# First batch's running sums on TensorE instead of VectorE scans, and the list of words written out anew

## The chip, the cores and the metric

The kernel runs on one core of one Trainium2 chip. A core has five engines that run their own instruction lists in order and wait for one another by semaphores: TensorE (matrix products, PE in the profile, with its weight loads PEld), VectorE (DVE), ScalarE (ACT), GpSimd (POOL) and SyncE (SP), which here issues most DMA transfers. The metric is the device time of one execution in microseconds; the median of three runs of the kernel before is 524.56 us (524.19 to 525.32).

## The reference

Two blocks follow one another, all in float32, with 4 batches, 8 heads of 48 channels and 768 tokens.

```python
f = 1.0 / (1.0 + np.exp(-f_logit))
for t in range(S):
    state = f[:, :, t, :, None] * state + np.einsum('bhd,bhe->bhde', k[:, :, t], v[:, :, t])
    y[:, :, t] = np.einsum('bhd,bhde->bhe', q[:, :, t], state)
x = y.transpose(0, 2, 1, 3).reshape(4, 768, 384)
u = x + np.real(np.fft.fft(np.fft.fft(x, axis=1), axis=2))
un = (u - u.mean(-1)) / sqrt(u.var(-1) + 1e-6)
out = u + np.maximum(un @ w_ch1, 0.0) @ w_ch2        # 384 -> 1536 -> 384
```

So each head is a gated linear recurrence with a decay for every channel and token, and then come a Fourier mixing over tokens and channels and a feed-forward block with a residual.

## The kernel before, in words

**Attention.** The work is cut into 16 units: unit u is one batch and two heads (batch u // 4), with the channels of both heads on 112 partitions and the 768 tokens along the row. A unit is treated in 6 chunks of 128 tokens. What the recurrence needs is, for each channel, the running sum of ln(1 + exp(-f)) over the tokens of a chunk, started anew at each chunk at -10. In `attention` (line 364 on) ScalarE makes the logarithm (lines 372, 373); VectorE's scan of line 379 makes the running sum W over the whole row, where the tile `bound` (22 everywhere, -10 at a chunk's first token) is the second operand of its `min` and so restarts the sum; line 380 adds the last token's logarithm and keeps the total of each chunk in `deep`. ScalarE takes exp(-W) and exp(W) (383, 384), and VectorE multiplies them into the queries and the keys (391, 392). Then come, on TensorE: the scores inside half chunks (`sc`, line 400), masked by VectorE into `at` (404); the scores between halves (576), copied to `ao`; the transposed keys (`st`, 538); the outputs `y` from scores and values (559); the state sums of each chunk (`ds`, 599), scanned over chunks by VectorE (`stt`, 607); the read-out of the state into `y` (616); and the transposition of the output (`yt`, 636), which ScalarE copies to the token-major x. VectorE folds x for the Fourier mixing (`fold`, 663 to 669; after the second and fourth unit of a batch also `xs`, `se`, `xc`, `ce`, 678 to 687).

**Mixing and feed-forward.** For each batch `fnet` makes four products `z` with the cosine and sine tables (724) and three `mix` products (743); each row block is normalised, transposed (`pt`, 782) and put through the feed-forward block in three pairs of row blocks. The first batch uses plain products: `up` (871, twelve for a pair, each with a relu on ScalarE), then `po` (880); its other two pairs and all later ones use a seven-product form for the second matrix (`fx`, `fz`, 894), and later batches a fifteen-product form for the first one (`ub`, 840). The two weight matrices arrive as float64 in 24 blocks: a word `r` fetches one (310), a word `C` turns it into float32 with one ScalarE, two VectorE and one GpSimd instruction (281 to 285). Three fetched blocks have room at a time, so a fetch waits for the GpSimd addition three blocks earlier.

**What sets the order.** Nothing is scheduled by the machine: the string `ORDER` is a list of words that is read from left to right, and each word emits a piece of the program, which every engine gets in this order. A number is the next step of that unit (its generator's next `yield`), K its transposed keys, L a load on SyncE's queue, F and H steps of the mixing, P a step of the feed-forward block, T and S the tables' loads and sorting, V and c a second reading of the weights for their smallest sizes, M the final test of whether the fast path was accurate. A word `D` emits eight products of the tile `bound` with itself into a spare part of the `y` tile (lines 189 to 194, 192): nobody reads them, they only occupy TensorE. The kernel before has 21 of them, 20 before the first z product.

**Buffers.** f, q and k tiles are shared by units (`home`), scores, keys, states and outputs take turns in two double banks of PSUM (`ps_a`, tag sc), the mixing in two banks (`ps_f`, tag f), and all units write to one `y`.

## Time and profile before

| | |
|---|---|
| median of three runs | 524.56 us (524.19 to 525.32) |
| profiled execution, first to last instruction | 526.3 us |
| mean granted TensorE clock | 0.974 |
| TensorE matmuls busy | 494.9 us (94%) |
| TensorE weight loads busy | 453.4 us (86%) |
| VectorE busy | 378.3 us (72%) |
| ScalarE busy | 218.4 us (42%) |
| GpSimd busy | 58.8 us (11%) |
| dummy products (line 192) | 14.6 us |
| scans of line 379 | 28.0 us, 16 of them |
| first z product of the first batch | at 59.5 us |

The profile is of one execution, and its span lies 1.7 us above the median of the runs, which are not profiled. Busy shares are means over stages with different limits: they are read stage by stage. A float32 product of the program stands as two matmul records in the trace, a transpose as one. "Issue" in the chain of waits is time in which an engine waited for nothing that the profile shows. The granted clock is 1.00 at full speed and 0.50 at half.

### The profile page before, as it was taken

The page shows a single profiled execution, that of the slowest core. Times are in us where ns is not written, and L with a number is a line of the kernel's source. Part 1 is how long each engine was busy: PE and PEld are TensorE (multiplying, and loading weights), DVE is VectorE, ACT ScalarE, POOL GpSimd, SP SyncE. Part 2 cuts the span into 40 slices and gives each one's busy share as a digit, 9 for nine tenths or more (in the row PEclk, how much of TensorE's full clock was granted, in tenths as well). Part 3 has the DMA queues.
Part 4 walks back from the last instruction along what each step waited for, and adds up shares of the span by engine and source line. Part 5 has one row for each costly group of instructions (what it writes and reads, how often), then busy time and mean ns, then how long its engine had stood idle before and what let it go on. Part 6 is the DMA issues. An engine that isn't in the chain of part 4 may idle for free.

```text
span 526.3 us, 13807 instructions
## 1 busy us (share of the span) xinstructions
PE 494.9 (94%) x5854; PEld 453.4 (86%) x5854; DVE 378.3 (72%) x746; ACT 218.4 (42%) x520; POOL 58.8 (11%) x85
## 2 busy tenths in 40 slices
PE   5878599999999999999999999999999999999994
PEld 4757388866899889999999999999999999999994
DVE  3598989989955368688588776779776667465571
ACT  5567368656331542453435523550431404031220
POOL 3045033551001000000001000000001000010100
PEclk9789699999999999999999999999999999999998
DMA  8957837575010230103212012120610312220200
GB/s 222 268 147 206 210 109 214 161 221 158 6 55 30 68 97 17 54 21 114 77 55 84 1 55 72 46 63 23 206 43 15 107 47 81 83 91 8 84 11 27
DMA packets 20650, 48.15 MB, mean 91 GB/s; under 512 B 3426, under 2 KB 6179, under 8 KB 20579
## 3 DMA queue, kind: packets, MB, share of 16 engines
q1 hardware_dynamic: 19474, 43.63, 29.5%
q0 software_dynamic: 1104, 3.54, 1.8%
q8 instruction: 48, 0.79, 0.6%
q14 instruction: 24, 0.19, 0.1%
HBM read 42.44 MB, written 4.72 MB: 90 GB/s over the span
## 4 chain that ended last, share of the span: by engine, by line
PE 87%; DVE 6%; issue 2%; ACT 2%; DMA 1%; POOL 0%; SPq 0%; DVEq 0%; ACTq 0%
PE ub L840 23%; PE fx L894 16%; PE fz L894 11%; PE up L871 9%; PE z L724 5%; PE y L559 4%; PE mix L743 3%; PE y L616 2%; PE sc L400 2%; PE ds L599 2%; PE po L880 2%; PE yt L636 2%; PE pt L782 1%; PE st L538 1%; PE y L192 1%
## 5 line engine op out<-in xcount | busy, mean ns | idle before, releaser
L849 DVE TENSOR_TENSOR h<-h,ub 128x512 f32<-128x512 f32 x81 | 55.2, 687 | 33.5 <-PE ub L840 24.5
L692 POOL DMA_INDIRECT out_dram<-x,place x16 | 16.4, 1024 | 357.6 <-DVE x L944 224.3
L847 ACT ACTIVATE h<-ub 128x512 f32<-128x512 f32 x54 | 31.9, 591 | 42.3 <-PE ub L840 42.3
L871 PE MATMUL up<-unT,w 128*128 128x256 f32 x216 | 49.4, 382 | 0.0
L840 PE MATMUL ub<-wide,w 128*128 128x128 f32 x360 | 45.0, 276 | 2.3 <-DVE wide L814 2.3
L894 PE MATMUL fx<-block,h 128*128 128x192 f32 x264 | 46.9, 328 | 0.0
L894 PE MATMUL fx<-w,h 128*128 128x192 f32 x264 | 45.5, 327 | 0.0
L840 PEld LDWEIGHTS ub<-wide,w 128*128 128x128 f32 x360 | 42.4, 192 | 3.4 <-PE pt L782 1.3
L871 PEld LDWEIGHTS up<-unT,w 128*128 128x128 f32 x216 | 40.1, 190 | 5.9 <-ACT h L873 0.4
L851 ACT ACTIVATE h<-h 128x512 f32<-128x512 f32 x45 | 28.4, 631 | 38.1 <-DVE h L849 37.7
L894 PEld LDWEIGHTS fx<-block,h 128*128 128x128 f32 x264 | 43.2, 190 | 0.5 <-DVE x L911 0.2
L894 PEld LDWEIGHTS fx<-w,h 128*128 128x128 f32 x264 | 42.7, 190 | 0.4 <-issue 0.2
L285 POOL TENSOR_TENSOR w<-w,raw 128x384 uint32<-128x384 uint32 x24 | 29.4, 1228 | 72.3 <-DVE w L284 39.1
L840 PE MATMUL ub<-unT,w 128*128 128x128 f32 x288 | 37.0, 275 | 0.0
L840 PEld LDWEIGHTS ub<-unT,w 128*128 128x128 f32 x288 | 34.6, 192 | 0.0
L783 ACT COPY unT<-pt 128x384 f32<-128x384 f32 x24 | 11.4, 484 | 46.8 <-PE pt L782 46.6
L840 PE MATMUL ub<-unT,wide 128*128 128x128 f32 x216 | 29.1, 278 | 0.0
L840 PE MATMUL ub<-wide 128*128 128x128 f32 x216 | 28.6, 275 | 0.1
L873 ACT ACTIVATE h<-up 128x256 f32<-128x256 f32 x36 | 13.9, 385 | 33.6 <-PE up L871 22.0
L840 PEld LDWEIGHTS ub<-unT,wide 128*128 128x128 f32 x216 | 26.4, 192 | 0.5
L840 PEld LDWEIGHTS ub<-wide 128*128 128x128 f32 x216 | 26.3, 192 | 0.3 <-PE ub L840 0.3
L379 DVE TENSOR_TENSOR_SCAN W<-g,bound 112x768 f32<-112x768 f32 x12 | 21.0, 1747 | 6.7 <-ACT g L373 6.7
(194 smaller groups left out, 1000.1 us busy)
## 6 DMA issues: line engine op xcount, KB each, us to landing
raw<-in_w_ch_dram SPq DMA_DIRECT2D x24, 384.0 KB, 5.1
v<-in_v_dram SPq DMA_DIRECT2D x16, 288.0 KB
k<-in_w_ch_dram SPq DMA_DIRECT2D x12, 384.0 KB, 3.4
g<-in_w_ch_dram SPq DMA_DIRECT2D x12, 384.0 KB, 3.3
k<-in_qkf_dram SPq DMA_DIRECT2D x14, 288.0 KB
g<-in_qkf_dram SPq DMA_DIRECT2D x12, 288.0 KB, 3.5
q<-in_qkf_dram SPq DMA_DIRECT2D x12, 288.0 KB, 3.3
wide<-in_qkf_dram SPq DMA_DIRECT2D x10, 288.0 KB, 4.7
```

The lines of the kernel that those rows point to most:

```text
L285: nc.gpsimd.tensor_tensor(bits, bits, lo, ALU.add)
L379: nc.vector.tensor_tensor_scan(W, g, bound[:R], 0.0, ALU.add, ALU.min)
L559: nc.tensor.matmul(y[FILL[g], c // 3, c % 3 * C + t.start:c % 3 * C + t.stop], lhsT=vals[rows, o:o + (64 if g == 0 else D)], rhs=weights, ...
L692: nc.gpsimd.indirect_dma_start(out=out.rearrange("b s d -> (b s) d"), out_offset=bass.IndirectOffsetOnAxis(ap=place[:, b, i:i + 1], axis=0 ...
L724: nc.tensor.matmul(z[:, cols], lhsT=src[:, j, lo:hi], rhs=tab[:, t, T % 2, cols], start=(i == 0), stop=(i == len(parts) - 1), skip_group_c ...
L743: nc.tensor.matmul(mix[:, o], lhsT=zz[:rows_of[T], T, PLACES[c]], rhs=cd[:rows_of[T], T, :NQ - odd], start=(i == 0), stop=(i == 1))
L840: nc.tensor.matmul(chains[chain][:, m * 128:(m + 1) * 128], lhsT=block(w)[:, m * 128:(m + 1) * 128], rhs=tokens(a), start=(new and m == 0) ...
L847: nc.scalar.activation(out, got, kind, scale=1.0 if how == "=+" else -1.0)
L849: nc.vector.tensor_tensor(out, out, got, ALU.add if how == "+" else ALU.subtract)
L851: nc.scalar.activation(out, out, AF.Relu)
L871: nc.tensor.matmul(pp[:, :256], lhsT=w1[:, kt, m * 128:(m + 1) * 128], rhs=unT[:, kt], start=(kt == 0), stop=(kt == 2))
L894: nc.tensor.matmul(out, lhsT=h[:, m], rhs=blocks[i][:, m], start=(start and m == 0), stop=(m == H - 1), skip_group_check=True)
```

## The change

For the first four units (the first batch) the running sums are made on TensorE. The exponential of f is transposed chunk by chunk into PSUM (`pg`, six transposes in a group of four and a group of two), ScalarE reads it there and writes the logarithm of one plus it token-major into `early["logs"]`, and one product for each chunk with a 128x128 triangle of ones (`early["upto"]`) gives the running sums channel-major in PSUM (`run`). Both exponentials read them there, with the offset of -10 as their bias (`low`, and the new tile `rise` with +10); VectorE only adds -10 to the six chunk totals. The triangle and the logarithms lie in the room that the feed-forward block's h uses later. Units 4 to 15 keep the scan.

Many steps are cut finer by added `yield`s (the two products of queries and keys, the fold, the mixing, the sums ahead of the fifteen products, the relu behind them), so the list has 961 words instead of 720, in another sequence. Of the `D` words four are left, two at the start, one among unit 3's steps and one in the third batch. The identity is loaded as the second transfer.

```diff
-    "L0f Z I 0 L0q L2q D D L1f L0k D 0 D 0 i D 1 L2f 2 0 D D D L0v 0 L1k K0 D 0 0 D L1q 0 1 D r 1 L3fk D "
...
+    "L0f E 0 i I L1f L2f D 1 0 D 1 2 L0q 0 0 0 L1k 1 0 0 2 L0k 0 L0v Z 1 1 0 0 r 2 L1q K0 1 C 0 1 1 2 0 0 "
...
+    rise = fixed([128, 1], "rise")
...
+        nc.gpsimd.memset(rise, -LOW)
...
+    def prefix():
+        room = ph1.tile([128, NF, 2, 128], F32, tag="h1", name="early").rearrange("p m t n -> p (m t n)")
+        early["upto"] = room[:, :C]
+        early["logs"] = room[:, C:C + HP * NCH * R].rearrange("p (u c k) -> p u c k", u=HP, k=R)
+        nc.gpsimd.memset(early["upto"], 1.0)
+        nc.gpsimd.affine_select(out=early["upto"], in_=early["upto"], pattern=[[1, C]], compare_op=ALU.is_ge,
+                                fill=0.0, base=0, channel_multiplier=-1)
...
         nc.scalar.activation(g, g, AF.Exp, scale=-1.0, accum_out=hot[:R, u:u + 1])
-        nc.scalar.activation(g, g, AF.Ln, bias=1.0)
-        yield
...
+        if u < HP:
+            yield
+            logs, run = early["logs"][:, u], []
+            for first, n in ((0, 4), (4, 2)):
+                pt = ps_f.tile([128, 512], F32, tag="f", name=f"pg{u}_{first}")
+                for c in range(n):
+                    nc.tensor.transpose(pt[:, c * R:(c + 1) * R], g[:, (first + c) * C:(first + c + 1) * C],
+                                        ident[:R, :R])
+                nc.scalar.activation(logs[:, first:first + n].rearrange("p c k -> p (c k)"), pt[:, :n * R],
+                                     AF.Ln, bias=1.0)
+                if first == 0:
+                    yield
+            yield
+            sum_of = ps_a.tile([128, 2, 512], F32, tag="sc", name=f"run{u}")
+            for c in range(NCH):
+                nc.tensor.matmul(sum_of[:R, c // 3, c % 3 * C:c % 3 * C + C], lhsT=logs[:, c], rhs=early["upto"],
+                                 start=True, stop=True)
+            nc.vector.tensor_scalar(T.rearrange("p (b c) -> p b c", b=2), sum_of[:R, :, C - 1:3 * C:C], LOW, None, ALU.add)
+            yield
+            W = p2.tile([128, S], F32, tag="W", name=f"W{u}")[:R]
+            halves = lambda a: a.rearrange("p (b n) -> p b n", b=2)
+            nc.scalar.activation(halves(g), sum_of[:R, :, :3 * C], AF.Exp, scale=-1.0, bias=rise[:R])
+            nc.scalar.activation(halves(W), sum_of[:R, :, :3 * C], AF.Exp, bias=low[:R])
+        else:
+            nc.scalar.activation(g, g, AF.Ln, bias=1.0)
...
         nc.vector.tensor_tensor(Q, Q, g, ALU.mult)
+        yield
         nc.vector.tensor_tensor(g, W, K, ALU.mult)
...
             for i, one, two, sign in made:
                 add(tokens(i), tokens(one), tokens(two), sign)
+            if made:
+                yield
...
             if complete and not first:
+                yield
                 nc.scalar.activation(out, out, AF.Relu)
```

The order in which the engines get their work changes at three places that matter below. In these listings a number behind a name (`sc1_0`: unit 1) tells the unit, and a row gives line, operation, what is written, what is read, the shape and how often.

On VectorE, the start of the program. Before, three scans stand ahead of unit 1's mask:

```order
L379 SCALAR_TENSOR_TENSOR W0_178<-g0_85,bound_96 112x768
L380 TENSOR_TENSOR deep_97<-g0_85,W0_178 112x6
L391 TENSOR_TENSOR q0_89<-q0_89,g0_85 112x768
L392 TENSOR_TENSOR g0_85<-W0_178,k0_87 112x768
L404 COPY_PREDICATED at0_91<-causal_95,sc0_0_237 128x768
L379 SCALAR_TENSOR_TENSOR W1_352<-g1_86,bound_96 112x768
L380 TENSOR_TENSOR deep_97<-g1_86,W1_352 112x6
L379 SCALAR_TENSOR_TENSOR W2_400<-wide_84,bound_96 112x768
L380 TENSOR_TENSOR deep_97<-wide_84,W2_400 112x6
L607 SCALAR_TENSOR_TENSOR stt0_403<-ds0_341,te0_98 112x288
L391 TENSOR_TENSOR q1_90<-q1_90,g1_86 112x768
L392 TENSOR_TENSOR g1_86<-W1_352,k1_88 112x768
```

Now:

```order
L419 TENSOR_SCALAR deep_97<-run0_180 112x6
L445 TENSOR_TENSOR q0_89<-q0_89,g0_85 112x768
L447 TENSOR_TENSOR g0_85<-W0_188,k0_87 112x768
L419 TENSOR_SCALAR deep_97<-run1_223 112x6
L459 COPY_PREDICATED at0_91<-causal_95,sc0_0_234 128x768
L305 TENSOR_SCALAR w1_107<-raw0_260 128x384
L306 SCALAR_TENSOR_TENSOR w1_107<-raw0_260,w1_107 128x384
L445 TENSOR_TENSOR q1_90<-q1_90,g1_86 112x768
L447 TENSOR_TENSOR g1_86<-W1_231,k1_88 112x768
L419 TENSOR_SCALAR deep_97<-run2_308 112x6
L664 SCALAR_TENSOR_TENSOR stt0_355<-ds0_341,te0_98 112x288
```

The scans and their sums are gone; two weight blocks are converted in the room between.

On TensorE, behind unit 0's state sums (`ds0`). Before, six sets of dummies, 48 products (`bound`), stand ahead of unit 1's scores:

```order
L599 MATMUL ds0_341<-v0_233,kT0_270 48x48x2
L192 MATMUL y_82<-bound_96 128x128
L400 MATMUL sc1_0_429<-q1_90,g1_86 64x64 x24
L616 MATMUL y_82<-q0_89,stt0_403 48x128 x10
L538 MATMUL st1_483<-ident_110,g1_86 128x112 x5
```

Now:

```order
L656 MATMUL ds0_341<-v0_208,kT0_274 48x48x2
L593 MATMUL st1_363<-ident_111,g1_86 128x112 x5
L673 MATMUL y_82<-q0_89,stt0_355 48x128 x10
L455 MATMUL sc1_0_396<-q1_90,g1_86 64x64 x24
L694 MATMUL yt0_423<-ident_111,yT0_382 128x112 x6
L407 MATMUL pg3_0_435<-ident_111,wide_84 128x112 x4
L407 MATMUL pg3_4_453<-ident_111,wide_84 128x112 x2
```

The dummies are gone; the scores stand behind the transposed keys and unit 0's read-out, and unit 3's transposes follow.

On VectorE, behind the fold that makes `se`, on which the first z product waits; ahead of these rows stand the rest of that fold, unit 4's state scan and unit 5's mask. Now (units 4 and 5 already have their scores' operands, units 6 and 7 get theirs here):

```order
L305 TENSOR_SCALAR w1_107<-raw3_886 128x384
L306 SCALAR_TENSOR_TENSOR w1_107<-raw3_886,w1_107 128x384
L432 SCALAR_TENSOR_TENSOR W7_1142<-wide_84,bound_96 112x768
L433 TENSOR_TENSOR deep_97<-wide_84,W7_1142 112x6
L432 SCALAR_TENSOR_TENSOR W6_1147<-wide_84,bound_96 112x768
L433 TENSOR_TENSOR deep_97<-wide_84,W6_1147 112x6
L664 SCALAR_TENSOR_TENSOR stt5_1218<-ds5_1185,te1_99 112x288
L445 TENSOR_TENSOR wide_84<-wide_84 112x768 x2
L447 TENSOR_TENSOR wide_84<-W7_1142,k1_88 112x768
L447 TENSOR_TENSOR wide_84<-W6_1147,k0_87 112x768
```

Before, the operands of units 4 and 5 and three weight blocks stood here, and units 6 and 7 came after the mixing.

More of the change, by code (lines that the diff above doesn't have):

```diff
@@ L371, in attention @@
         AT, AO = at_t[u % 2], ao_t[u % 2]
+        T = deep[:R, u]
         nc.scalar.activation(g, g, AF.Exp, scale=-1.0, accum_out=hot[:R, u:u + 1])
-        nc.scalar.activation(g, g, AF.Ln, bias=1.0)
-        yield
-        T = deep[:R, u]
-        W = p2.tile([128, S], F32, tag="W", name=f"W{u}")[:R]
-        nc.vector.tensor_tensor_scan(W, g, bound[:R], 0.0, ALU.add, ALU.min)
-        nc.vector.tensor_tensor(T, home("f", u)[:R, C::C], W[:, C - 1::C], ALU.add)
-        yield
-        nc.scalar.activation(g, W, AF.Exp, scale=-1.0)
@@ L384, in attention @@
-        nc.scalar.activation(W, W, AF.Exp)
+        if u < HP:
[24 more added lines that the diff above has]
+            yield
+            W = p2.tile([128, S], F32, tag="W", name=f"W{u}")[:R]
+            nc.vector.tensor_tensor_scan(W, g, bound[:R], 0.0, ALU.add, ALU.min)
+            nc.vector.tensor_tensor(T, home("f", u)[:R, C::C], W[:, C - 1::C], ALU.add)
+            yield
+            nc.scalar.activation(g, W, AF.Exp, scale=-1.0)
+            nc.scalar.activation(W, W, AF.Exp)
@@ L679, in fold @@
         if last:
+            yield
             eo_of.pop(b)
@@ L792, in turns @@
                 else:
-                    turn(step)
+                    yield from turn(step)
                 yield
@@ L861, in projected @@
             if again:
-                for _ in range((3, 3, 2)[j]):
+                for _ in range((5, 5, 4)[j]):
                     next(behind[b], None)
@@ L1017 @@
                 sort_tables(wave)
+            elif kind == "E":
+                prefix()
             elif kind == "Z":
```

12 lines of the change are left out of this document (added), and 45 rows, old and new, of the table ORDER.

## The prediction

> **What bounds the kernel now.** I read first the busy time by stage (columns: stretch in us, its length, then busy us of TensorE matmuls, weight loads, VectorE, ScalarE and GpSimd with their instructions, granted clock, DMA share, GB/s), and then the same view for the dummy products of line 192 alone.
>
> ```profile
> 0.00:26.00 26.00, 17.14 (x357) 15.90 (x361) 11.17 (x13) 15.28 (x24) 4.80 (x29) 0.87 0.95 247
> 26.00:59.50 33.50, 22.63 (x595) 18.67 (x587) 30.74 (x57) 21.51 (x53) 13.35 (x20) 0.83 0.75 198
> 59.50:78.70 19.20, 18.93 (x300) 14.49 (x300) 16.49 (x34) 9.60 (x30) 4.78 (x5) 0.84 0.42 111
> 78.70:150.50 71.80, 70.54 (x975) 56.48 (x974) 66.94 (x108) 43.61 (x105) 20.96 (x17) 1.00 0.51 146
> 150.50:519.40 368.90, 365.61 (x3644) 347.85 (x3642) 252.61 (x536) 128.43 (x308) 14.87 (x15) 1.00 0.20 60
> 519.40:526.30 6.90, 0.03 (x1) 0.00 (x0) 0.36 (x1) 0.00 (x0) 0.00 (x0) 0.75 0.16 48
> ```
>
> ```profile
> 0.00:26.00 26.00, 11.25 (x128) 10.65 (x128) 0.87 0.95 247
> 26.00:59.50 33.50, 2.75 (x32) 2.29 (x32) 0.83 0.75 198
> 59.50:78.70 19.20, 0.61 (x8) 0.53 (x8) 0.84 0.42 111
> ```
>
> From 59.5 us on TensorE is idle for 0.3, 1.3 and 3.3 us in the three stages up to 519.4. Ahead of 59.5 it does 39.8 us, of which 14.0 are dummies: 25.8 us of wanted work, 33.7 us without. So what the change can win lies in the first 59.5 us, and work that is pulled into them leaves the full part behind. The chain of waits (start us, length, what) and VectorE's own rows tell what holds this head:
>
> ```profile
> 20.17 4.87 PE y L192 x48
> 25.04 0.90 PE sc L400 x48
> 26.90 1.76 DVE W L379
> 59.54 8.37 PE z L724 x28
> 150.58 3.90 PE fx L894 x24
> ```
>
> ```profile
> 20.23 0.76 DVE L607 TENSOR_TENSOR_SCAN stt<-ds,te 112x288 f32<-112x288 f32 x1 [2.82 <-PE ds L599]
> 25.96 1.04 DVE L404 COPY_PREDICATED at<-causal,sc 128x768 f32<-128x768 uint32 x1 [3.08 <-PE sc L400]
> 28.68 0.17 DVE L380 TENSOR_TENSOR deep<-wide,W 112x6 f32<-112x6 f32 x1
> 28.77 0.35 DVE L283 TENSOR_SCALAR w<-raw 128x384 uint32<-128x384 uint32 x1
> 29.16 0.56 DVE L284 SCALAR_TENSOR_TENSOR w<-raw,w 128x384 uint32<-128x384 uint32 x1
> 29.63 0.95 DVE L391 TENSOR_TENSOR wide<-wide 112x768 f32<-112x768 f32 x1
> 58.98 0.46 DVE L681 TENSOR_TENSOR se<-xs 128x285 f32<-128x285 f32 x1
> ```
>
> Up to 26 us two things hold: loads (DMA share 0.95) and 48 dummies, which the in-order TensorE queue runs at 20.17 ahead of unit 1's scores, so that VectorE waits 3.08 us for them. From 26 to 59.5 VectorE is busy 30.74 of 33.5 us, and the first z product starts 0.1 us behind the fold that makes `se` (the row of 58.98). VectorE is the bound there.
>
> **The change part by part.** *VectorE, up to the fourth fold.* I count its list between unit 1's mask (`at`) and `se`, in both programs. The change has one scan with its sum fewer (1.76 + 0.17), three weight blocks fewer (3 x 0.91), four 112x768 products more (units 4 and 5, 4 x 0.95), one mask more (1.04), and a sum of six values read from PSUM, not in this trace, between 0.17 (its SBUF form) and 0.4; I take 0.2. Together +0.4 us. What goes is ahead of that stretch: three of the four scans, and the 48 dummies. Unit 1's mask stood at 25.96; now its scores wait only for unit 0's state scan, five transposes and one read-out.
>
> ```profile
> 12.44 0.70 PE L538 MATMUL st<-ident,g 112*128 112x112 f32 x5
> 225.44 0.89 PE ub L840 x8
> 234.56 0.84 PE y L616 x20
> L847 ACT ACTIVATE h<-ub 128x512 f32<-128x512 f32 x54 | 31.9, 591 | 42.3 <-PE ub L840 42.3
> ```
>
> *The running sums on TensorE.* Neither form stands in the trace, so I price them by neighbours, three pieces of the chain and a group of the page, above. Transposes: five for 0.70, six for 0.84. A product with 128 columns of float32: eight records, which are four products of the program, for 0.89; six for 1.33. So 2.2 us of TensorE a unit, 8.7 us for four. The logarithm read from PSUM (448 and 224 columns) has no row: its bounds are 0.59 us for 512 columns above, and two thirds of it for the pair below; I take 0.9 us for both, against 0.84 for the logarithm that goes. Exponentials from PSUM I leave at their 0.84. Unit 0 then gets its sums after 0.84 + 0.9 + 1.33 = 3.1 us where logarithm and scan took 0.84 + 1.76 = 2.6, so its state scan stays at about 20.3. Behind it 0.84 for the read-out and 0.90 for unit 1's scores, some waiting: mask at 22.7, 3.3 us earlier. First z product: 59.5 - 3.3 + 0.4 = **56.6**. Lower bound 54 (VectorE without its 2.8 idle us), upper 59.5 (loads hold the units as now; the queue of loads has the same bytes ahead).
>
> *Work pulled ahead of z.* The 8.7 us lie in the 33.7 without wanted work, in the room of 12 us of dummies that go. If that cover were gone they would cost 8.7. Moreover units 4 and 5 come earlier: unit 4's keys, scores, both output parts and state sums and unit 5's keys and scores stand before the second z. By these rows and those above:
>
> ```profile
> 13.72 0.57 PE L559 MATMUL y<-at,v 64*48 64x64 f32 x24
> 14.09 0.55 PE L576 MATMUL sc<-q,g 48*64 48x64 f32 x24
> 228.29 0.85 PE y L559 x45
> 229.14 0.78 PE ds L599 x16
> ```
>
> 2 x 0.70 + 2 x 0.90 + 0.57 + 0.55 + 0.85 + 0.78 = 5.95 us that TensorE no longer does between z and the first fx product (150.58). In exchange unit 9's read-out (0.84) is now ahead of fx: counted there, it is missing behind. TensorE's work ahead of z is 25.8 + 8.7 + 5.95 = 40.4 us in 56.6.
>
> *Clock.* The four z products took 8.37 us at half clock; batch 1's take 1.30 + 3.94:
>
> ```profile
> 178.22 1.30 PE z L724 x6
> 182.29 3.94 PE z L724 x22
> 16.00:26.00 10.00, 7.75 (x142) 7.23 (x139) 3.97 (x6) 5.35 (x9) 0.00 (x0) 0.66 1.02 268
> 54.00:66.00 12.00, 7.25 (x23) 4.82 (x24) 11.21 (x27) 4.58 (x15) 0.00 (x0) 0.57 0.75 200
> ```
>
> With more wanted work just ahead of z the clock may be full there: between 0 and -3.1. I take -3.1 and make the next part's waits at full clock too; if z runs at half clock again, TensorE comes later and waits less by as much, so the choice moves the sum little.
>
> *New waits behind z.* VectorE's list from `se` to unit 6's keys (it ends with the third listing) is: rest of the fold 2.3, two state scans 1.5, a mask 1.04, a weight block 0.91, two scans with sums 3.9, four products 3.8 = 13.4 us, so 56.6 + 0.4 + 13.4 + 0.5 = 70.9. TensorE has 12.7 us to do before unit 6's scores (z 5.24, read-outs 1.68, unit 5's outputs and states 2.75, one yt 0.7, mid and first mix 1.6, one st 0.7): it comes there at 69.3 and stands 1.6 us; queued behind are st6, the second mix and unit 5's yt. With unit 6's mask and its read-out, where the same list goes on, I take 3 us in all; between 0 and 6. The second place is the last weight block (four pieces of the chain, and VectorE's row):
>
> ```profile
> 111.14 1.02 POOL w L285
> 112.18 4.41 DMA raw<-in_w_ch_dram
> 105.34 1.31 PE up L871 x6
> 106.65 1.94 PE po L880 x6
> 116.61 0.36 DVE L283 TENSOR_SCALAR w<-raw 128x384 uint32<-128x384 uint32 x1 [0.96 <-DMA raw<-in_w_ch_dram]
> ```
>
> An up of three products is 1.31, three products of po 1.94. VectorE had 47.9 us of list work between `se` and that block and needed 57.2; the changed list has 52, and with 8 over it (some of the 9.3 were waits for the slow z) it is there at 57 + 60 = 117, the GpSimd addition at 118. TensorE wants the block 23.0 us of work after z starts (to the first up), 3 us of waits, and 33.5 us of work later (twelve ups, nine products of po, the parts of units 6, 7 and 9 between): 116.1. So 2 us more; between 0 and 5.
>
> *End.* Before, TensorE stood between the last ub and fx while the maximum over the weights was judged:
>
> ```profile
> 490.69 12.76 PE ub L840 x112
> 505.59 4.10 PE fx L894 x24
> ```
>
> 503.45 to 505.59 is 2.1 us. The changed list judges one pair earlier, behind an fx product whose last addition it must await (about 0.9): -1.2. One set of dummies stands in the third batch: +0.6.
>
> **Sum**, against the span of 526.3: -2.9 (z) - 5.95 - 0.85 - 3.1 + 3.0 + 2.0 - 1.2 + 0.6 = -8.4, span 517.9. The median of the runs, 524.56, lies 1.7 below the span; I carry that over: **516.2 us**. The lower bounds together (z at 54, no new waits) give 508.6.
>
> **Rivals.** *The clock stays down in the head* (slower). 136 dummies that kept TensorE busy go, and half of the new instructions are transposes. Place: from about 12 us to z, some 37 us of work; price: 8.37 / 5.24 = 1.6, so 59 us, z at 71. Then +11.5 - 5.95 - 0.85 - 0.6 = +4.1 and no new waits: 528.7. It decides once z comes after 67, with about seven tenths of that stretch at half clock. For it: 0.66 and 0.57 in the two rows above, with dummies. Against it: dense work brings the clock back (18.93 of 19.2 us busy at 59.5, and full clock before 67), and the changed list is denser.
> [...]
>
> *The weights set the pace.* The fetches run three deep and each waits for the GpSimd addition three blocks before. If the last block comes at 121, fx starts at 121 + 1.0 + 26.3 (the rest of po, twelve ups and unit 8's scores) = 148.3, and the sum is -2.3 - 0.85 - 0.6 = -3.7: 520.8. For it: VectorE waits 0.96 us for that load already; against it: DMA share of only 0.51 there.
>
> *All of it counts:* no new waits: 516.2 - 5.0 = 511.2.
>
> *It wins nothing:* the finer words reorder the dense part, which loses only 3.3 us now; 7 us lost there and the head's gain is gone: 524.5.
>
> That the scans were no bound after all, loads hold, and z stays at 59.5 would not change much: the 5.95 us are still pulled ahead and VectorE has time for the new waits (-5.95 - 0.85 - 3.1 + 2 - 0.6 = -8.5). This case belongs to the forecast.
>
> **Chances.** Forecast 0.45, all of it counts 0.17, weights 0.16, nothing 0.08, clock 0.14. A measurement of this kernel tells about 0.2% from no change. Faster: 0.45 + 0.17 + 0.16 + 0.02 = 0.80; within 0.2%: 0.06; slower 0.14. The likeliest alone spans 513 to 519; eight in ten, from the lower bound to the edge of the clock case, 508.5 to 525.5.
>
> **What would show it.** The first z product at 55 to 58 and unit 1's mask at 22 to 24 in VectorE's rows; no line 192 beyond 2.5 us; fx of batch 0 at 143 to 147; TensorE waiting at unit 6's scores near 70 and at po near 118; a gap under 1.2 us before the last fx. Wrong, if the clock of 26:59.5 falls below 0.7, or if TensorE loses over 8 us between 150 and the end.

## The result and the profile after

The changed kernel takes 518.52 us (median of four executions, 517.25 to 519.38), the kernel before 524.94 us beside it (524.19 to 525.9): ratio 0.9874, 95% interval 0.985 to 0.9898. The forecast was 516.2 us, 508.5 to 525.5. In two later groups of runs, both on one chip, the changed kernel took 518.95 and 518.59 us, beside 526.95 and 525.82 us of the kernel before. Of the experiments below, the ratio of e3 leaves out two disturbed executions of its six, and one of these is the profiled one, so that its rows show the place of a loss and not its size.

The profiled execution has a span of 515.4 us and a mean granted clock of 0.995 (before: 526.3 and 0.974). Busy time by stage, cut as in the prediction, and then the dummy products alone (their line is now 214):

```profile
0.00:26.00 26.00, 18.74 (x322) 16.25 (x323) 9.00 (x15) 17.28 (x36) 7.70 (x34) 1.00 0.94 238
26.00:59.50 33.50, 26.15 (x805) 21.67 (x803) 29.43 (x57) 22.61 (x55) 9.59 (x17) 1.00 0.94 241
59.50:78.70 19.20, 18.30 (x418) 14.80 (x417) 18.75 (x34) 16.34 (x48) 5.46 (x4) 1.00 0.42 133
78.70:150.50 71.80, 69.82 (x666) 55.26 (x666) 66.84 (x114) 38.37 (x92) 22.27 (x18) 1.00 0.48 138
150.50:508.50 358.00, 355.55 (x3587) 340.58 (x3585) 246.40 (x525) 121.64 (x296) 15.70 (x15) 1.00 0.19 59
```

```profile
0.00:26.00 26.00, 2.09 (x16) 1.71 (x16) 1.00 0.94 238
26.00:59.50 33.50, 0.62 (x8) 0.45 (x8) 1.00 0.94 241
```

The clock column reads 1.00 in each stage, where it read 0.87, 0.83 and 0.84 in the first three. The trace's clock records begin only at 11.9 us, though (at 7.4 us before); the column counts the time ahead of them as 1.00, and the products there took 1.7 to 1.8 times their later time (last section). DMA is now busy 0.94 of the stage from 26 us on (0.75 before). Ahead of 59.5 us TensorE does 44.9 us, of which 2.7 are dummies: 42.2 us of wanted work, where it was 25.8.

Where the 10.9 us between the two spans lie is seen when both profiles are cut at the first z product and at the first fx product of the first batch. Before:

```profile
0.00:59.54 59.54, 39.77 (x940) 34.60 (x941) 41.94 (x69) 36.78 (x77) 18.15 (x49) 0.85 0.84 220
59.54:150.58 91.04, 89.55 (x1272) 71.03 (x1273) 83.39 (x141) 53.21 (x135) 25.73 (x21) 0.97 0.49 138
150.58:519.40 368.82, 365.53 (x3643) 347.77 (x3642) 252.61 (x536) 128.43 (x308) 14.87 (x15) 1.00 0.20 60
```

After:

```profile
0.00:57.23 57.23, 42.62 (x1099) 36.36 (x1099) 36.16 (x68) 39.29 (x86) 17.29 (x51) 1.00 0.94 240
57.23:143.54 86.31, 83.43 (x1063) 64.67 (x1064) 82.75 (x144) 54.30 (x140) 27.73 (x22) 1.00 0.51 151
143.54:508.50 364.96, 362.51 (x3631) 347.52 (x3630) 251.51 (x533) 122.65 (x298) 15.70 (x15) 1.00 0.19 58
```

Up to z: -2.3 us. From z to fx: -4.7 us, of which TensorE's busy time gives -6.1 and its idle time, 1.5 before and 2.9 now, takes back 1.4. From fx to the end of TensorE's work: -3.9 us, of which 3.0 are busy time. The tail behind it is 6.9 us in both.

The steps of the head, in VectorE's rows (unit 1's mask, the fold that makes `se`) and in TensorE's (first z product):

```profile
24.52 1.05 DVE L459 COPY_PREDICATED at<-causal,sc 128x768 f32<-128x768 uint32 x1 [0.97 <-PE sc L455]
56.68 0.45 DVE L742 TENSOR_TENSOR se<-xs 128x285 f32<-128x285 f32 x1
```

```profile
57.23 1.51 PE L786 MATMUL z<-tab,se 128*95 128x385 f32 x6 [1.89 <-issue]
59.51 1.54 PE L786 MATMUL z<-tab,xs 128*96 128x385 f32 x6
```

The mask is 1.4 us earlier than before (25.96), z 2.3 us, and z runs at full clock: 1.51 us for six records, 2.85 before. The chain of waits now goes through loads and weight blocks up to the last products of po:

```profile
49.33 5.63 DMA k<-in_qkf_dram
...
111.85 3.44 DMA raw<-in_w_ch_dram
...
117.11 1.02 POOL w L307
118.17 8.65 PE po L948 x26
...
143.54 1.95 PE fx L962 x12
```

That these loads are on the chain doesn't mean that TensorE stands for them: at po it waited 0.2 us (below).

Prices of the new instructions, from the groups of the first 60 us (line, engine, operation, out<-in, shapes, count | busy us, mean ns of one record):

```profile
L417 PE MATMUL run<-early 128*112 128x128 f32 x48 | 7.6, 315 | 0.7 <-ACT early L409 0.7
L407 PE MATMUL pg<-ident,g 112*128 112x112 f32 x12 | 3.0, 402 | 2.4 <-ACT g L395 2.4
L407 PE MATMUL pg<-ident,wide 112*128 112x112 f32 x12 | 1.8, 271 | 0.0
L409 ACT ACTIVATE early<-pg 128x448 f32<-128x448 f32 x4 | 2.2, 540 | 0.7 <-PE pg L407 0.7
L409 ACT ACTIVATE early<-pg 128x224 f32<-128x224 f32 x4 | 1.4, 354 | 0.0
L424 ACT ACTIVATE g<-run,rise 112x768 f32<-112x768 f32 x2 | 1.8, 902 | 2.0 <-DVE deep L419 2.0
```

TensorE pays 12.4 us for the four units' sums (8.7 were forecast); the logarithm from PSUM takes 0.89 us for both pieces (0.9); the exponential from PSUM takes 0.90 us (left at 0.84).

### The profile page after: what moved, and what is told of

Same layout as the page of the kernel before. It is cut to its first block, busy times and chain, and to the rows that moved or that the text cites. A ratio compares the mean times of both kernels' runs of the same rounds, so it can differ in the third digit from the quotient of the medians.

```text
span 515.4 us, 13694 instructions
## 1 busy us (share of the span) xinstructions
PE 488.6 (95%) x5790; PEld 448.6 (87%) x5790; DVE 370.4 (72%) x742; ACT 216.2 (42%) x524; POOL 60.7 (12%) x88
## 4 chain that ended last, share of the span: by engine, by line
PE 76%; DMA 12%; DVE 7%; SPq 1%; issue 1%; POOL 1%; ACT 1%; DVEq 0%; ACTq 0%; POOLq 0%
PE ub L907 24%; PE fx L962 17%; PE fz L962 13%; PE up L939 6%; DMA raw<-in_w_ch_dram 4%; PE z L786 3%; PE mix L805 2%; DMA wide<-in_qkf_dram 2%; DMA k<-in_qkf_dram 2%; DMA g<-in_qkf_dram 2%; PE y L614 2%; PE po L948 2%; DMA v<-in_v_dram 1%; PE yt L694 1%; DVE w L306 1%
## 5 line engine op out<-in xcount | busy, mean ns | idle before, releaser
L754 POOL DMA_INDIRECT out_dram<-x,place x16 | 17.6, 1100 | 346.3 <-DVE x L1012 160.7
L907 PE MATMUL ub<-wide,w 128*128 128x128 f32 x360 | 44.9, 276 | 2.0 <-DVE wide L879 1.9
L907 PEld LDWEIGHTS ub<-wide,w 128*128 128x128 f32 x360 | 42.5, 192 | 2.8 <-issue 1.6
L846 ACT COPY unT<-pt 128x384 f32<-128x384 f32 x24 | 11.4, 474 | 32.1 <-PE pt L845 32.1
L962 PE MATMUL fz<-w,s 128*128 128x192 f32 x132 | 23.4, 327 | 0.0
L962 PE MATMUL fz<-block,h 128*128 128x192 f32 x132 | 23.4, 327 | 0.0
```

The costliest lines, as they stand in the source:

```text
L754: nc.gpsimd.indirect_dma_start(out=out.rearrange("b s d -> (b s) d"), out_offset=bass.IndirectOffsetOnAxis(ap=place[:, b, i:i + 1], axis=0 ...
L846: nc.scalar.copy(turned[j][:, :, t], pt[:, :DM].rearrange("p (k t) -> p k t", k=3))
L907: nc.tensor.matmul(chains[chain][:, m * 128:(m + 1) * 128], lhsT=block(w)[:, m * 128:(m + 1) * 128], rhs=tokens(a), start=(new and m == 0) ...
L962: nc.tensor.matmul(out, lhsT=h[:, m], rhs=blocks[i][:, m], start=(start and m == 0), stop=(m == H - 1), skip_group_check=True)
```

## The experiments

Each group of four kernels ran on one chip together with the kernel before: e1 to e4 on one chip, the other two groups on another. All times are medians in us. The changed kernel ran in the second and the third group.

| kernel | median | beside the changed kernel | ratio to the kernel before (95%) |
|---|---|---|---|
| e1, scans back | 521.65 | | 0.9897 (0.9872 to 0.9922) |
| e2, old list, no dummies | 530.43 | | 1.0069 (1.0039 to 1.0099) |
| e3, sums in the old list | 546.1 | | 1.032 (1.027 to 1.037) |
| e4, sums of units 4 and 5 too | 532.19 | | 1.0108 (1.0066 to 1.0149) |
| e7, changed kernel again | 518.95 | 0 | 0.9856 (0.9816 to 0.9895) |
| e8, scans back again | 521.73 | +2.8 | 0.9897 (0.9862 to 0.9932) |
| e5, sums of 4 and 5, placed later | 522.39 | +3.4 | 0.9913 (0.9877 to 0.9949) |
| e6, old list, gap filled | 527.44 | | 0.9995 (0.9971 to 1.0019) |
| e12, changed kernel, third time | 518.59 | 0 | 0.9864 (0.9822 to 0.9906) |
| e9, 48 dummies back | 523.37 | +4.8 | 0.9966 (0.994 to 0.9993) |
| e10, warm start | 521.34 | +2.7 | 0.9898 (0.9865 to 0.9931) |
| e11, warm start and gaps | 520.97 | +2.4 | 0.9898 (0.9854 to 0.9941) |

**What the sums alone are worth: scans back in the new list (e1, e8).**

```diff
-            logs, run = early["logs"][:, u], []
-            ... transposes, logarithms, products of the sums, six totals
+            nc.scalar.activation(g, g, AF.Ln, bias=1.0)
+            yield
+            yield
+            W = p2.tile([128, S], F32, tag="W", name=f"W{u}")[:R]
+            nc.vector.tensor_tensor_scan(W, g, bound[:R], 0.0, ALU.add, ALU.min)
+            nc.vector.tensor_tensor(T, home("f", u)[:R, C::C], W[:, C - 1::C], ALU.add)
```

> The changed kernel, with scans for the first four units again, in the new list of words at the places of the sums. Theory A (VectorE's list sets the first z product, and the sums on TensorE take 7 us out of it): the four scans bring 4 x 1.8 = 7 us back to VectorE, of which some 3 to 5 lie where it is busy. Unit 1's mask at 25 to 27 instead of 24.5, first z at 60 to 62 instead of 57.2, median 521.5 to 523.5 against 518.5. Rival B (the list alone does it: dummies gone, work of units 4 and 5 pulled ahead of z): the same 518.5 within 0.7, the 12 us of transposes and products saved on TensorE being in its idle time.

> The changed kernel with scans for the first four units once more, beside the changed kernel on the same chip. If the sums on TensorE are worth what the first z product moved (4.2 us), it is 4 us slower than the changed kernel; if most of it is taken back by later waits (weights, unit 6), 1 us or less.

> The changed kernel itself, on the same chip as the next three, so that they are compared with it directly. If the profile of the kernel before (span 526.3, granted clock 0.974) was one of its slower executions, its other executions have spans 1.75 us under their times and lie at 523 to 527, and the changed kernel's spans at 515 to 518.

Beside the changed kernel on the same chip the scans cost 2.8 us (e8 against e7), between the two values expected of e8; of the 8.0 us that the change gave on that chip, 5.2 stay without the sums. VectorE's rows of unit 1's mask and of the fold that makes `se`, in e8:

```profile
24.26 1.03 DVE L446 COPY_PREDICATED at<-causal,sc 128x768 f32<-128x768 uint32 x1 [0.97 <-PE sc L442]
60.22 0.45 DVE L729 TENSOR_TENSOR se<-xs 128x285 f32<-128x285 f32 x1
```

The same two in e1, with the scan between them, and then TensorE's transposes of unit 0's output in e1:

```profile
26.51 1.06 DVE L446 COPY_PREDICATED at<-causal,sc 128x768 f32<-128x768 uint32 x1 [2.37 <-PE sc L442]
31.81 1.74 DVE L407 TENSOR_TENSOR_SCAN W<-wide,bound 112x768 f32<-112x768 f32 x1
60.91 0.45 DVE L729 TENSOR_TENSOR se<-xs 128x285 f32<-128x285 f32 x1
```

```profile
26.58 1.38 PE L681 MATMUL yt<-ident,yT 112*128 112x112 f32 x6 [0.23 <-ACT yT L674]
```

In e8 the mask is not late (24.70 in e7), although three scans stand ahead of it. `se` is 3.2 us late (57.00 in e7), and so is z (60.77 and 57.55). Between mask and `se` VectorE is busy for 30.1 us instead of 28.2, which is the one scan with its sum that the prediction counted there, and it waits for 5.8 us instead of 4.1. So theory A names the place rightly, but not the whole price.

The other 1.7 us go with TensorE's pace, which no expectation had: the sums also keep TensorE busy at the start. The trace's clock records begin, with full clock, at 11.9 us in the changed kernel (12.1 in e7, 11.4 in e12), but at 22.1 us in e8, where the clock is at half again from 25.5 to 42.6, and at 42.5 us in e1. That e1's products ran at half pace until then is seen in their durations only: the six transposes above take 1.38 us, in the changed kernel 0.79, though the clock column of e1 reads 1.00 throughout the head. There the mask is late as well, behind slow scores. How much of the 2.8 us is VectorE's scan and how much TensorE's pace was not separated.

Behind z the two kernels are alike: from z to fx 86.8 us in e8 and 87.1 in e7, from fx to the end of TensorE's work 365.4 and 365.1. So what the sums give lies ahead of z, and what the new list gives by itself lies behind it: there e8 is 4.3 and 3.4 us shorter than the kernel before, although its z comes 1.2 us later. Rival B, that the list does all of it, falls too. Which part of the list does its share (dummies gone, units 4 and 5 ahead, finer words) was not separated.

**The sums in the old list (e3).** The kernel before with the four units' sums on TensorE, transposes in the step of the logarithm, products in the step of the scan, dummies kept.

```diff
+        if u < HP:
+            logs = early["logs"][:, u]
+            ... transposes into pg, logarithms from PSUM
+            yield
+            ... products with the triangle, totals
+            yield
+            ... both exponentials from PSUM
```

> The kernel before, dummies and list of words kept, with the sums of the first four units on TensorE (transposes in the step of the logarithm, products in the step of the scan; the identity and the triangle first). Theory A: three of the four scans stood ahead of unit 1's mask, which the dummies hold, so VectorE gains only one scan where it is the bound, and TensorE has 12 us more in a queue that still holds 14 us of dummies: first z at 58 to 60, median 523.5 to 526. Rival D (the sums by themselves make the gain): first z at 56 to 57, median 519 to 521.

Slower by 3.2%, far outside both expectations. VectorE's wait for unit 0's scores:

```profile
21.87 1.04 DVE L437 COPY_PREDICATED at<-causal,sc 128x768 f32<-128x768 uint32 x1 [7.03 <-PE sc L433]
```

Unit 0's mask stood at 12.62 us before. TensorE takes its list in order, and unit 0's scores now stand behind the transposes of units 1 and 2 and 24 dummies; the transposes wait for those units' exponentials, which ScalarE makes behind unit 0's. The same instructions that are worth 2.8 us in a list written for them cost some 17 us in one that is not.

**The dummies of the old list (e2, e6).** In e2 all 21 words D are taken out of the old list; in e6 five are added ahead of the first z product.

```diff
-    "... L0q L2q D D L1f L0k D 0 D 0 i D 1 L2f 2 0 D D D ..."
+    "... L0q L2q L1f L0k 0 0 i 1 L2f 2 0 ..."
```

> The kernel before without its dummy products (all 21 words D), nothing else. Theory A (the dummies stand on the path: 48 of them hold unit 1's scores): unit 1's mask 2 to 3 us earlier than 25.96, first z at 57 to 58, median 522 to 523 against 524.9. Rival C (they kept the clock up, or the head's clock goes by wanted work alone and stays down): granted clock under 0.8 from 26 to 59.5 and the z products at half clock, no gain or slower, 525 to 528. If the clock is 1.00 there without them, they were what pulled it down.

```diff
-    "... L6fk 3 2 3 5 R 3 F0 F0 ..."
+    "... L6fk 3 2 3 5 R 3 D D D D D F0 F0 ..."
```

> The kernel before with five more words of eight dummy products each, just ahead of the first z product, where TensorE stands idle for 4.4 us. Theory G (the clock halves where TensorE stands idle for over some 2 us, whatever fills the rest): clock 1.00 from 54 to 66, the four z products in 5.2 to 5.5 us instead of 8.4, first z where it was, 2 to 3 us faster than the kernel before. Rival: the clock goes by how much wanted work there is, or falls at that place for another reason: z stays at 8 us, no gain, or up to 2 us slower because 40 dummies at half clock take 4.1 us.

Without dummies the old list is 0.7% slower, more than rival C allowed (525 to 528 us). Unit 1's mask does come earlier (24.23 against 25.96), as theory A says. But the trace's clock records begin with full clock only at 29.0 us (7.4 in the kernel before), and from 42.6 us on the clock is at half again, behind TensorE's longest wait; this wait and two stages of e2:

```profile
43.90 1.53 PE L616 MATMUL y<-wide,stt 48*48 48x128 f32 x20 [3.94 <-DVE stt L607]
```

```profile
42.00:54.00 12.00, 8.09 (x150) 6.95 (x151) 7.17 (x12) 5.61 (x13) 6.75 (x12) 0.57 0.76 194
54.00:66.00 12.00, 6.48 (x36) 4.31 (x37) 10.68 (x27) 4.31 (x13) 0.00 (x0) 0.60 0.66 185
```

In the kernel before the stage from 42 to 54 us has clock 1.00, and three words D lie in it. Without them the clock is lost there, which is rival C, and first z came at 61.59, 2 us late. In e6 the added dummies brought nothing:

```profile
61.09 1.80 PE L724 MATMUL z<-tab,se 128*95 128x385 f32 x6 [2.14 <-issue]
62.68 2.77 PE L724 MATMUL z<-tab,xs 128*96 128x385 f32 x6
```

2.1 of the 4.4 us of idle time were left, the clock was 1.00 from 52 to 62 us and fell then, so that the second product ran at half pace; another such stretch, from 48 to 52 us, had made `se` 1.5 us late. Theory G in its simple form (fill most of the idle time and the clock stays) falls. The 2 us of idle time that it names were the author's estimate; no run shows such a bound (last section).

**Dummies back in the new list (e9).**

```diff
         own = ps_a.tile([128, 2, 512], F32, tag="sc", name=f"sc{u}_0")
+        if u == 1 and few[0]:
+            for _ in range(6):
+                busy()
```

> The changed kernel with 48 dummy products put back just ahead of unit 1's scores, where the kernel before has them; nothing else. Theory A (they stand on the path to unit 1's mask, and from there VectorE's list sets z): 48 x 56 ns = 2.7 us, so mask at 27.3 instead of 24.6, first z 2 to 3 us later than 57.4, 1.5 to 3 us slower than the changed kernel. Rival (what comes behind has slack, VectorE idling some 4 us between 26 and 59.5, or the loads hold it): the mask moves by 2.7, z by under 1, the time by under 1.

4.8 us slower, more than the 2.7 us of their work. TensorE's row of the dummies, then VectorE's of unit 1's mask, then TensorE's of z:

```profile
26.19 2.84 PE L214 MATMUL y<-bound 128*128 128x128 bf16 x48 [1.15 <-ACT yT L690]
```

```profile
30.02 1.06 DVE L462 COPY_PREDICATED at<-causal,sc 128x768 f32<-128x768 uint32 x1 [5.10 <-PE sc L458]
```

```profile
62.79 1.51 PE L789 MATMUL z<-tab,se 128*95 128x385 f32 x6 [0.29 <-issue]
```

The mask is 5.3 us later than in the changed kernel beside it (24.68), z 5.3 us (57.48). From the mask to z it counts one to one, in spite of VectorE's 4 us of idle time between. The added wait of 1.15 us comes from the buffer: the dummies write into a spare part of `y`, and so wait until ScalarE has read unit 0's output from it. That part of their price the expectation had not seen. The remaining 1.3 us of the 5.3 are not the dummies' doing: in this execution the clock was at half from 16.6 to 20.0 us, ahead of them, so that unit 0's read-out already ran 1.4 us later than in the first profile of the changed kernel. How far the other executions lost the same is not known.

**More sums on TensorE (e4, e5).** In e4 units 4 and 5 get their sums on TensorE as well, in the two steps that they have; in e5 the transposes stand one step later, and the products with the exponentials.

```diff
-        if u < HP:
-            yield
+        if u < HP + 2:
+            if u < HP:
+                yield
```

> The changed kernel, with the sums of units 4 and 5 on TensorE as well (in the two steps that they have). Theory A (VectorE's list sets the first z product also in the changed kernel): two scans of 1.75 with their sums fewer between 34 and 45 us, 3.5 us less on VectorE's list, 6 us more on TensorE, which idles 14.6 us ahead of z: first z at 54 to 56 instead of 57.2, median 515.5 to 517.5 against 518.5. Rival E (the loads hold the head now, DMA share 0.94 from 26 to 59.5): z stays at 57 and the median at 518.5. Rival F (TensorE's in-order queue is the next bound): z later than 57.2, 519 to 521.

```diff
+        elif u < HP + 2:
+            yield
+            ... transposes and logarithms
+            yield
+            ... products, totals, both exponentials
-    "... 2 3 3 2 5 5 D 4 4 3 3 K4 ..."
+    "... 2 3 3 2 5 D 4 4 5 3 3 K4 ..."
```

> The changed kernel with the sums of units 4 and 5 on TensorE too, but with their transposes at the place of the scan and not at that of the exponential, so that TensorE does not stand for a load. Theory A (VectorE's list sets the first z product): 3.5 us less on VectorE between 34 and 45 us, no TensorE wait over 2 us, clock 1.00, first z at 54 to 56, 1 to 3 us faster than the changed kernel. Rival E (the loads hold the head): z at 57 and no difference. Rival F (TensorE's in-order queue is the bound once its idle time is spent): z at 58 or later, slower.

Both are slower: e4 by 2.5% of the time before (ratio 1.0108; the changed kernel's, in another group, 0.9856), e5 by 3.4 us. In e4 TensorE stands for unit 4's exponential, its clock is at half from 32.9 to 43.1 us, and VectorE stands behind it:

```profile
33.45 1.38 PE L408 MATMUL pg<-ident,g 112*128 112x112 f32 x6 [2.86 <-ACT g L395]
```

```profile
37.73 0.76 DVE L665 TENSOR_TENSOR_SCAN stt<-ds,te 112x288 f32<-112x288 f32 x1 [6.94 <-PE ds L657]
```

The expectation of e5 takes this for a load; ScalarE's rows show that the exponential only stands behind unit 3's two in its list. In e5 that wait is gone and the clock is 1.00 in the head from 11.9 us on. VectorE's rows of unit 5's totals, and of unit 4's mask, which stands behind them in its list:

```profile
49.87 0.16 DVE L443 TENSOR_SCALAR deep<-run 112x6 f32<-112x6 f32 x1 [2.63 <-PE run L441]
54.20 1.05 DVE L481 COPY_PREDICATED at<-causal,sc 128x768 f32<-128x768 uint32 x1
```

That mask came at 50.6 in the changed kernel beside it (e7). The scan needs VectorE alone once the logarithm is there, and unit 5's ended at 45.2 there. The new route goes from ScalarE into TensorE's list, back to ScalarE and to TensorE again, and in this list, where one step of unit 5 stands two words further back, it delivers unit 5's totals 4.6 us later; VectorE, freed of 3.5 us, stands for them in order, and z comes at 62.34. So theory A is right only as long as VectorE has its operands: with one scan fewer the next bound is the route of the unit itself. That is rival F, in a form that neither expectation had.

**A warm start (e10, e11).** In the changed kernel TensorE runs its first products at about half pace (twelve records of the sums in 2.77 us, later in 1.56), though the clock column says 1.00. Its dummies at the start and its first and third sets of products of the sums:

```profile
2.44 1.03 PE L214 MATMUL y<-bound 128*128 128x128 bf16 x8 [2.44 <-POOL rise L185]
8.90 2.77 PE L417 MATMUL run<-early 128*112 128x128 f32 x12
18.32 1.56 PE L417 MATMUL run<-early 128*112 128x128 f32 x12
```

e10 adds two words D ahead of unit 1's first step; e11 adds to that eight dummies ahead of unit 1's output transposes and sixteen ahead of z.

```diff
-    "L0f E 0 i I L1f L2f D 1 0 D 1 2 ..."
+    "L0f E 0 i I L1f L2f D D D 1 0 D 1 2 ..."
```

> The changed kernel with two more words of eight dummies ahead of unit 1's first step, so that TensorE works without a break from 2.4 us to the first transposes. Theory G (after idle time TensorE runs at half pace until it has worked for some microseconds, at the start too, where the clock's record still says 1.00): the first set of products of the running sums in 1.6 to 2.0 us instead of 2.77, transposes 0.8 instead of 1.38, unit 0's mask 1 to 2 us earlier than 16.0, unit 1's mask 0.5 to 1.5 earlier, the time 0 to 1.5 us shorter. Rival (the loads of k hold unit 0): unit 0's products faster, its mask where it was, no change of the time.

> The kernel of the run before, with eight dummies more where TensorE waits 1.1 to 1.6 us ahead of unit 1's output transposes, and sixteen in the 1.9 us ahead of the first z product. Theory G: TensorE's idle time falls under 1.2 us at each place, the granted clock is 1.00 from 11 us on in every execution, and the spread of the times, 4 us for the changed kernel, falls below 2 us; the median 0.5 to 2 us lower. Rival: dummies ahead of z delay it where VectorE comes early, or the clock falls elsewhere: no gain.

> The changed kernel once more, as the measure for the three runs beside it: 518 to 520, z at 57.0 to 57.8, one stretch of half clock or none ahead of z.

The start is warm as theory G says. In e10 (first the dummies, then the first and third sets of the sums):

```profile
2.43 2.74 PE L214 MATMUL y<-bound 128*128 128x128 bf16 x24 [2.43 <-POOL rise L185]
8.30 1.04 PE L417 MATMUL run<-early 128*112 128x128 f32 x8
9.93 0.69 PE L417 MATMUL run<-early 128*112 128x128 f32 x4 [0.58 <-ACT early L409]
18.40 2.90 PE L417 MATMUL run<-early 128*112 128x128 f32 x12
```

The first set takes 1.04 + 0.69 = 1.73 us instead of 2.77, and unit 0's mask is 1.0 us earlier (15.04). But then the clock falls, at a place where it is full in the changed kernel. The stage from 16 to 22 us of e10:

```profile
16.00:22.00 6.00, 6.00 (x93) 5.36 (x96) 2.95 (x6) 2.41 (x5) 1.22 (x1) 0.50 1.00 240
```

The third set takes 2.90 us, unit 1's mask comes at 26.16 (1.5 us late), z at 59.32 (1.8 us late), and the time is 2.7 us longer. e11 loses its clock from 23 to 30, from 44 to 51 and from 61 to 64 us and is 2.4 us longer; its times spread over 4.3 us and not below 2. No version beats the changed kernel.

## Why the prediction was right, and where it was not

The time lies 2.3 us above the forecast and within its range, and the mechanism, a head that ends earlier with TensorE's work pulled into it, is what the profiles show. That the number is so near is in part luck: several steps are off by 2 us and more, and cancel. By steps:

| step | forecast | measured |
|---|---|---|
| unit 1's mask | 22.7 | 24.5 |
| first z product | 56.6 (-2.9) | 57.2 (-2.3) |
| TensorE's wanted work ahead of z | 40.4 us | 39.9 to z, 42.2 to 59.5 |
| z at full clock | -3.1 | about -2.3 |
| TensorE's work taken out from z to fx (keys, scores, outputs, state sums; busy time by line) | -5.95 | -6.4 |
| new waits from z to fx | +5.0 | +1.4 |
| fx of batch 0 | 143 to 147 | 143.5 |
| from fx to the end | -1.45 | -3.9 |
| span | 517.9 | 515.4 |
| median below (-) or above (+) the span | -1.7 | +1.75 for each execution |

*Head.* From mask to `se` it took 33.0 us before and takes 32.2 now, where 0.4 more were forecast, and e9 shows that what delays the mask delays z one to one. The count of VectorE's instructions there was right, their sizes were not: VectorE is busy for 28.1 us instead of 30.3, and waits for 4.0 instead of 2.7. These two errors hid one another. The mask came 1.8 us later than forecast, because unit 0's transposes and products were priced with rows of full pace (0.84, 1.33) and ran at half pace (1.38, 2.77); unit 0's state scan, forecast at about 20.3, stands at 21.95. z missed by 0.6 us only, since the list behind the mask was shorter than counted. The attribution was half right: the sums give 2.8 us (e8 against e7) of some 8, and the rest belongs to the list that the change brings with it. The forecast let the mask come earlier because scans and dummies go; e8, with its scans, has its mask at 24.26, so that the scans ahead of the mask cost nothing there.

*Cover.* The sums cost 12.4 us of TensorE's time and not 8.7, and TensorE is idle for 14.6 us up to 59.5 even so. That this work would bring the full clock forward (11.9 us against 22.1 and 42.5 without it, e8 and e1) the prediction did not have.

*Clock.* z ran at full clock; 1.51 + 1.54 + 1.56 + 1.48 = 6.1 us instead of 5.24, with other work now between its four products. That makes 2.3 us and not 3.1.

*Pulled work.* This term held (table). TensorE's busy time as a whole fell by 6.1 us from z to fx, though, while the busy times of the single lines fell by 8.0 together: products of neighbouring lines overlap less than before.

*New waits.* This is the most mis-sized term ahead of fx: TensorE was to stand at unit 6 and at the last weight block, 3.0 and 2.0 us. TensorE waited for `mid` ahead of unit 6 and for the last block:

```profile
PE mid L820 <- issue: 0.7, 1, 0.7
PE po L948 <- POOL w L307: 0.2, 1, 0.2
```

The weights set part of the chain but were there in time (118.17; 118 was forecast), so that rival two didn't decide.

*Behind fx.* -0.85 was a slip of the sum: the read-out of unit 9 moves from behind fx to ahead of it, which gains nothing, and the term ahead of fx, +0.84, was left out of the sum; with it the forecast would have been 517.0. The 2.1 us at the judging of the weights were misread: the chain's step ends at 503.45, but TensorE's rows show `ub` products up to 504.5 and then a wait of 0.73 us only:

```profile
505.21 0.38 PE L969 MATMUL turned<-ident,most 128*1 128x128 f32 x2 [0.73 <-DVE most L967]
```

This wait is gone, as forecast, but the wait for the pair's sums grew from 0.94 to 1.30 us, so that some 0.4 us were won there and not 1.2. TensorE's rows now:

```profile
478.92 0.38 PE L1037 MATMUL turned<-ident,most 128*1 128x128 f32 x2
480.60 1.13 PE L907 MATMUL ub<-wide,w 128*128 128x128 f32 x8 [1.30 <-DVE wide L879]
```

Of the 3.0 us of TensorE's busy time saved behind fx, the read-out explains 0.85 and the added dummies take 0.6. The remaining 2.8 us, 0.8% of this part, were not forecast, and even the rival "it wins nothing" had the opposite sign. They belong to the list and not to the sums: they stand in two more profiles of the changed kernel (362.5 us of busy time) and in e1 and e8 with their scans (362.7), and not in e2 and e6, with the old list (365.7 and 365.5). Spread over some 3,600 records they are 0.8 ns each, and the groups' means don't show where they lie. What in the list does it was not tested.

*From span to median.* The carry-over was wrong. In every execution with both numbers the time is 1.7 to 2.0 us above its span, so the profiled execution of the kernel before, with its span of 526.3, took some 528, more than any of the four timed beside the changed kernel. The prediction took one of its slower executions as the base and then subtracted 1.7 where 1.75 had to be added. (e7 had expected spans of 523 to 527 us for the kernel before and of 515 to 518 for the changed one; they reach from 522.8 to 528.7 and from 516.5 to 520.7.) The spans differ by 10.9 us, the medians by 6.4. Waits 3.6 us too dear and an offset 3.5 us too low hid one another in part; this is the luck of the number.

*The clock as a rival.* It did not happen: the clock was 1.00 from 11.9 us on with 136 dummies fewer ahead of z and 24 transposes more. The rival names the transposes among the new instructions; no run here separates them from products. That the clock can go with the dummies is shown all the same. In the old list their loss does keep the clock down (e2: 0.57 from 42 to 54 us, where the kernel before has 1.00; 3.5 us slower); in the new list other work takes their place, the sums among it, and without the sums the head is at half pace for most of its first 42 us (e1, e8). And it is near: e10 loses 2.7 us, with half clock from 15.8 to 22.6 us behind a shift of 1 us.

## What to carry to other kernels

Work that is moved to an idle engine with an in-order list is worth only what the list lets it be: the same sums gave 2.8 us in a list written for them, and cost 3.2% in the old one and 3 to 13 us for two units more, because TensorE stood in order for ScalarE, and VectorE for both. Here it also had a second effect, on the engine's clock (without the sums e8 is at half clock from 25.5 to 42.6 us, where the changed kernel has 1.00), and a run that takes it away takes both. Before a profiled execution is used as the base, hold its time (span plus the constant that other executions show) against the spread of the runs, and say which one it was. In the head, where TensorE is not dense (44.9 us of 59.5), a shift of 1 us changed its clock (half from 15.8 to 22.6 us in e10; e10 and e11, built to keep it up, took 2.7 and 2.4 us more), so measure variants side by side on one chip, and read the pace from the durations of equal products, not from the clock column alone.

## What the runs showed of the hardware

*The clock and the spread.* The kernel before varies from 523.2 to 530.4 us, the changed one from 517.3 to 522.4. For the kernel before the time goes with the granted clock: of its 20 executions in the second group, those with a clock of 0.983 to 0.986 took 524.5 to 526.3 us, those with 0.973 to 0.977 took 526.3 to 530.4. For e1 it doesn't (0.996 and 522.9 us, 0.990 and 520.9), as the mean leaves out the time ahead of the first record.

*When the clock changes.* In the kernel before the record has stretches of 10.2, 6.8, 10.2, 6.8, 13.7 and 10.2 us, at full and half clock in turn from 7.4 us on, which are 3, 2, 3, 2, 4 and 3 times 3.41 us. In e10 and e11, read from their clock in slices of 2 us, the half stretches are 6.8, 3.4 and 3.4 us and 6.8, 6.8 and 3.4 us long. No length of a gap decides in these traces: 1.9 us ahead of z left the clock at 1.00 in the changed kernel and in e12, 1.55 us ahead of unit 1's output transposes was followed by half clock in e10 (from 36.2 us). What goes with it here is TensorE's busy share of the 3.41 us before (cut in such steps from a change of the clock, in the changed kernel and e12 from the record's first entry). In the kernel before, the changed kernel, e10, e11 and e12, up to 84 us, the clock fell nine times, behind stretches with 38 to 62% of busy time (51, 53 and 55% in the kernel before; 57, 52 and 38% in e10; 52, 62 and 47% in e11); two such stretches left it full, with 61% (e11, 33.5 to 36.9 us) and with 50% (e12, 55.8 to 59.2), and so did every one above 62%. It rose nine times, each time behind a stretch that was busy throughout.

*The first microseconds.* Up to about 11 us the changed kernel's products took 1.7 to 1.8 times their later time (8 dummies 1.03 us and later 0.62, twelve records of the sums 2.77 and 1.56; in e10 at a recorded clock of 0.50 these take 2.90), while the profile's clock reads 1.00: the record has no event there. In e1 this lasts up to 42.5 us. In e10, with 24 dummies in a row from 2.4 us on, it was over by 6.0 us: the next eight dummies, at 5.99, took 0.61 us, in the changed kernel at 6.29 1.06. Only the durations show it, not the clock column.

*A warm engine can be slower.* e10 is the case for it: faster first products, the next ones at half clock, 2.7 us lost. The clock fell there at 15.8 us, behind 3.41 us with 57% of busy time; from 11 to 16 us TensorE was busy for 3.2 us, in the changed kernel for 4.0. What makes this difference was not separated.

*A dummy has dependencies too.* Written into a part of a tile that nobody reads, it still waited 1.15 us for ScalarE's reading of the other part.
